# A quarter of the key sums of a decode attention moved from TensorE to ScalarE and VectorE

## The chip, the cores and the metric

The kernel runs on one core of one Trainium2 chip. The metric is device time in microseconds (us) of one execution, so lower is better. Each kernel was run several times, and one execution of each was recorded by the hardware profiler. All profile times below count from the first recorded instruction. The profiled span is some 1.8 to 2.1 us shorter than the device time of the same run.

## The reference

One token (D = 640) passes a pre-norm attention block and then a gated feed-forward block. The attention reads the last 4096 keys and values of 32 heads of 192 numbers, all in bfloat16.

```python
W = min(4096, max(256, Sk // 4))                 # 4096
q = (norm(x) @ wq).reshape(B, Sq, 32, 192).transpose(0, 2, 1, 3)
k = k_cache[:, :, Sk - W:, :]
v = v_cache[:, :, Sk - W:, :]
scores = jnp.einsum('bhqd,bhkd->bhqk', q, k) * Dh ** (-0.5)
o = jnp.einsum('bhqk,bhkd->bhqd', softmax(scores), v)
h = x + merge_heads(o) @ wo
z = gelu(norm(h) @ w_in)                         # 640 -> 1536, halves z1 and z2
out = h + (z1 * (w_sp * norm(z2) + b_sp)) @ w_out    # 768 -> 640
```

The caches that are read are 2 x 32 x 4096 x 192 x 2 bytes = 100.7 MB, and the weights some 18.7 MB more. Each byte is used once.

## The kernel before

A *pair* is two heads. The 16 pairs have one K tile and one V tile each, of 128 partitions x 12288 bfloat16 (3.1 MB). All loads are issued by one engine, SyncE, in one fixed order, and a load is issued when a buffer of its kind is free. There are six buffers for K and V together and two for wo.

```python
plan = [...wq..., K0, K1]
for t_ in range(NP):                                   # NP = 16 pairs
    if t_ + 2 < NP: plan.append(K[t_ + 2])
    if t_ % 2 == 1 and t_ < NP - 1: plan.append(wo[t_ // 2])
    plan.append(V[t_])
plan += [wo[7], w_in in 4 pieces, w_out in 6 pieces]
def free(kind, n=1):
    live[kind] -= n
    issue()                    # issues loads until the next one has no free buffer
```

The scores of a pair are made in two halves of 32 keys per partition. VectorE multiplies the keys by q in place, TensorE adds groups of products by matmuls with an identity matrix (12 for each half, 384 in all), and VectorE adds the last 16 columns of each key out of PSUM.

```python
def multiply(t, ch):           # VectorE, 128 x 6144 products
    nc.vector.tensor_tensor(out=kc, in0=kc, in1=q2[:, t:t + 1, :].to_broadcast([P, JC, Dh]), op=ALU.mult)

def contract(t, ch):           # TensorE; G = 16, NT = 12
    for n in range(NT):
        nc.tensor.matmul(psv, lhsT=ident_bf[:], rhs=k3[:, ch * JC:(ch + 1) * JC, n * G:(n + 1) * G],
                         start=(n == 0), stop=(n == NT - 1))
    if ch == NCH - 1:
        free("kv")             # the K buffer is free when TensorE has read it

def collect(t, ch):            # VectorE, 128 x 512 -> 128 x 32
    nc.vector.tensor_reduce(out=S[:, ch * JC:(ch + 1) * JC], in_=st[t]["ps"][ch], axis=AX.X, op=ALU.add)
```

Then come a maximum over the head (`head_max`), the exponentials on ScalarE (`exps`), the products with V on TensorE (`values`), the softmax sums Z of two pairs (`sums`, `norms`) and the projection with wo (`project`). The first six of the eight groups q of wo give rows of the result and the last two give columns. The stages of neighbouring pairs are interleaved:

```python
for t in range(NP):
    multiply(t, 0); collect(t - 1, 1); norms(...); multiply(t, 1)
    contract(t, 0); head_max(t - 1); scaled(t - 3); columns2(...)
    values(t - 2, vt, 0, J // 2); collect(t, 0); exps(t - 1, ...); project(...)
    contract(t, 1); values(t - 2, vt, J // 2, J); free("kv"); sums(...)
```

The *tail* after the loop handles the last two V tiles, adds the rows and x into columns (`fold`), and does the whole feed-forward block. Its end is this:

```python
    rstd2 = ln_rstd(hv2)       # start value, then two Newton steps, tiny VectorE instructions
    z2_ps = half_in(Fh)        # w_in, gelu, second norm with rstd3 = ln_rstd(hv3), ...
    nc.vector.tensor_tensor(out=gv[:], in0=z1[:], in1=gz[:], op=ALU.mult)
    for c in range(FHC):       # 6 pieces of w_out, 4 matmuls each
        for g in range(NG):
            nc.tensor.matmul(orow[...], lhsT=gv[:, c:c + 1], rhs=w_out_sb[:, c, g * OW:(g + 1) * OW], ...)
    nc.vector.tensor_copy(out=o_sb[:], in_=orow)      # the eviction
    nc.sync.dma_start(out=out[...], in_=o_sb[0::32, :])
```

## Time and profile before

| | before |
|---|---|
| device time | 287.45 us median of 4 runs (287.22 to 288.01) |
| profiled span | 285.7 us |
| packet time of the load queue | 97.4% of 16 engines' span = 278.3 us |
| PE, VectorE, ScalarE busy | 184.7, 193.0, 26.4 us |
| mean granted TensorE clock | 0.865 |

These are lines of the page of the kernel before. The first ones give the busy time of each engine, the granted clock in 40 slices, two DMA queues (packets, MB, share of 16 engines' span) and the chain that ended last, by engine. The L lines are groups of instructions: busy us and mean ns of one, then the idle time of the engine ahead of them and what ended most of it. The last two lines are loads: KB each and median us from issue to landing.

```profile
span 285.7 us, 3043 instructions
...
PE 184.7 (65%) x1245; PEld 77.2 (27%) x1245; DVE 193.0 (68%) x282; ACT 26.4 (9%) x98; POOL 2.3 (1%) x10
...
PEclk9999998889999579968997797978898679979555
...
q1 hardware_dynamic: 5544, 119.35, 97.4%
q8 instruction: 10, 0.16, 0.2%
...
DMA 59%; PE 20%; DVE 19%; issue 1%; SPq 1%; DVEq 0%
...
L299 PE MATMUL sc_ps<-k_t,ident_bf 128*128 128x512 bf16 x384 | 109.0, 445 | 45.6 <-DVE k_t L293 45.6
L293 DVE TENSOR_TENSOR k_t<-k_t,q_203 128x6144 bf16<-128x6144 bf16 x32 | 107.2, 3353 | 35.9 <-DMA k_t<-in_A_k_cache_dram 35.9
...
L332 ACT ACTIVATE E_125<-S,bias 128x64 bf16<-128x64 f32 x12 | 4.2, 360 | 73.8 <-DVE bias L326 73.8
...
k_t<-in_A_k_cache_dram SPq DMA_DIRECT2D x15, 3072.0 KB, 31.4
v_t<-in_A_v_cache_dram SPq DMA_DIRECT2D x15, 3072.0 KB, 31.6
...
```

The load queue q1 is busy 97.4% of the span, and no engine has more than 68%. VectorE waits 35.9 us in all for K tiles (group L293), so in the loop the arithmetic waits for the data. A K load lands 31.4 us after its issue.

The end of the chain of waits before, in order of time (start, us, what):

```profile
...
264.60 11.96 DMA w_in_sb<-in_B_w_in_dram
...
276.57 5.74 DMA w_out_sb<-in_B_w_out_dram
...
282.35 0.33 PE sc_ps L572 x4
...
282.71 0.33 DVE o_sb L575
```

At the end the chain runs along loads: the last landing of w_out at 276.57 + 5.74 = 282.31 us releases the last four matmuls, and the eviction of the result starts at 282.71 us. The rest, eviction and store, takes 2.8 to 3.0 us in every kernel here. So the start of the eviction is a good measure of the end, and I use it below.

### The profile page before, as it was taken

What the parts mean: (1) busy time and instruction counts of PE and PEld (TensorE: products, weight loads), DVE (VectorE), ACT (ScalarE), POOL (GpSimd) and SP (SyncE); (2) the same over time, 40 slices, a digit from 0 to 9 for tenths busy, and PEclk for the clock granted to TensorE, in tenths of its full rate; (3) what the DMA queues carried; (4) which work ended last, traced back from release to release, by engine and by line L of the source; (5) the groups of instructions that cost most, each with busy time, mean ns of one, the idle gap of its engine ahead of it and who ended that gap; (6) DMA issues with size and microseconds to landing.
All of it is one profiled execution on the core that took longest, in us unless ns stands there. A gap on an engine that the chain in (4) does not pass through costs nothing.

```text
span 285.7 us, 3043 instructions
## 1 busy us (share of the span) xinstructions
PE 184.7 (65%) x1245; PEld 77.2 (27%) x1245; DVE 193.0 (68%) x282; ACT 26.4 (9%) x98; POOL 2.3 (1%) x10
## 2 busy tenths in 40 slices
PE   1229948779765766736573866655772776776973
PEld 0003413223222322312231322212221222323562
DVE  7300088989996849587595939595786849986342
ACT  2001200101102010201002010201010010202211
POOL 3000000000000000000000000000000000000000
PEclk9999998889999579968997797978898679979555
DMA  8999999999999999999999999999999999999992
GB/s 330 406 434 434 434 440 416 421 452 440 443 434 406 440 420 434 420 463 440 434 429 414 420 440 428 445 445 440 427 411 417 434 434 418 479 434 390 394 403 95
DMA packets 5564, 119.54 MB, mean 418 GB/s; under 512 B 1005, under 2 KB 2286, under 8 KB 2990
## 3 DMA queue, kind: packets, MB, share of 16 engines
q1 hardware_dynamic: 5544, 119.35, 97.4%
q8 instruction: 10, 0.16, 0.2%
q14 instruction: 4, 0.03, 0.0%
q10 hardware_dynamic: 6, 0.00, 0.0%
HBM read 119.34 MB, written 0.00 MB: 418 GB/s over the span
## 4 chain that ended last, share of the span: by engine, by line
DMA 59%; PE 20%; DVE 19%; issue 1%; SPq 1%; DVEq 0%
DMA k_t<-in_A_k_cache_dram 35%; DVE k_t L293 13%; PE sc_ps L299 12%; DMA v_t<-in_A_v_cache_dram 11%; DMA wq_t<-in_A_wq_dram 7%; PE sc_ps L265 5%; DMA w_in_sb<-in_B_w_in_dram 4%; DVE ob L395 2%; DMA w_out_sb<-in_B_w_out_dram 2%; DVE S L307 2%; PE pv_169 L370 1%; SPq L60 1%; PE sm_ps L317 1%; PE attn_ps L428 1%; DVE gm L319 0%
## 5 line engine op out<-in xcount | busy, mean ns | idle before, releaser
L299 PE MATMUL sc_ps<-k_t,ident_bf 128*128 128x512 bf16 x384 | 109.0, 445 | 45.6 <-DVE k_t L293 45.6
L293 DVE TENSOR_TENSOR k_t<-k_t,q_203 128x6144 bf16<-128x6144 bf16 x32 | 107.2, 3353 | 35.9 <-DMA k_t<-in_A_k_cache_dram 35.9
L299 PEld LDWEIGHTS <-ident_bf 128*128 128x128 bf16 x384 | 41.2, 111 | 104.0 <-issue 63.3
L265 PE MATMUL sc_ps<-wq_t,xn_128 128*128 128x512 bf16 x60 | 18.3, 467 | 10.8 <-DMA wq_t<-in_A_wq_dram 8.4
L307 DVE TENSOR_REDUCE S<-sc_ps 128x32 f32<-128x512 f32 x32 | 21.9, 683 | 1.9 <-PE sc_ps L299 1.9
L273 DVE COPY sp_f<-sm_ps 128x2 f32<-128x2 f32 x1 | 0.2, 159 | 26.6 <-PE sm_ps L271 26.6
L265 PEld LDWEIGHTS <-xn_128 128*128 128x128 bf16 x60 | 6.7, 112 | 22.1 <-issue 15.0
L332 ACT ACTIVATE E_125<-S,bias 128x64 bf16<-128x64 f32 x12 | 4.2, 360 | 73.8 <-DVE bias L326 73.8
L332 ACT ACTIVATE E_127<-S,bias 128x64 bf16<-128x64 f32 x10 | 3.5, 363 | 67.0 <-DVE bias L326 67.0
L332 ACT ACTIVATE E_126<-S,bias 128x64 bf16<-128x64 f32 x10 | 3.5, 362 | 66.7 <-DVE bias L326 66.7
L319 DVE TENSOR_REDUCE gm<-sm_ps 2x1 f32<-2x128 f32 x16 | 4.5, 278 | 7.6 <-PE sm_ps L317 7.6
L370 PE MATMUL pv_169<-v_t,E_127 128*8 128x512 bf16 (+1 forms) x72 | 7.9, 489 | 1.9 <-DMA v_t<-in_A_v_cache_dram 1.9
L370 PE MATMUL pv_171<-v_t,E_126 128*8 128x512 bf16 (+1 forms) x72 | 6.2, 425 | 1.1 <-DMA v_t<-in_A_v_cache_dram 1.1
L267 ACT ACTIVATE q_203<-sc_ps 128x512 bf16<-128x512 f32 x6 | 3.6, 597 | 29.9 <-PE sc_ps L265 29.9
L370 PE MATMUL pv_169<-v_t,E_125 128*8 128x512 bf16 (+1 forms) x72 | 6.2, 425 | 0.0
L370 PEld LDWEIGHTS <-E_127 128*8 128x8 bf16 (+1 forms) x120 | 3.5, 87 | 8.1 <-issue 6.0
L370 PE MATMUL pv_171<-v_t,E_125 128*8 128x512 bf16 (+1 forms) x48 | 4.2, 424 | 1.5 <-DMA v_t<-in_A_v_cache_dram 1.5
L370 PE MATMUL pv_171<-v_t,E_127 128*8 128x512 bf16 (+1 forms) x48 | 4.1, 424 | 1.3 <-DMA v_t<-in_A_v_cache_dram 1.3
L370 PEld LDWEIGHTS <-E_125 128*8 128x8 bf16 (+1 forms) x120 | 3.2, 84 | 6.3 <-issue 3.6
L370 PEld LDWEIGHTS <-E_126 128*8 128x8 bf16 (+1 forms) x120 | 3.2, 84 | 6.0 <-issue 3.3
L370 PE MATMUL pv_169<-v_t,E_126 128*8 128x512 bf16 (+1 forms) x48 | 4.2, 425 | 0.0
L326 DVE TENSOR_TENSOR bias<-off,sm_ps 128x2 f32<-128x2 f32 x16 | 2.4, 148 | 2.5 <-PE sm_ps L324 2.5
(225 smaller groups left out, 141.5 us busy)
## 6 DMA issues: line engine op xcount, KB each, us to landing
k_t<-in_A_k_cache_dram SPq DMA_DIRECT2D x15, 3072.0 KB, 31.4
v_t<-in_A_v_cache_dram SPq DMA_DIRECT2D x15, 3072.0 KB, 31.6
wq_t<-in_A_wq_dram SPq DMA_DIRECT2D x5, 1536.0 KB, 14.2
wo_t<-in_A_wo_dram SPq DMA_DIRECT2D x7, 960.0 KB, 20.3
k_t<-in_A_k_cache_dram SPq DMA_DIRECT2D x1, 1536.0 KB
v_t<-in_A_v_cache_dram SPq DMA_DIRECT2D x1, 1536.0 KB
w_in_sb<-in_B_w_in_dram SPq DMA_DIRECT2D x2, 576.0 KB, 14.4
wo_t<-in_A_wo_dram SPq DMA_DIRECT2D x2, 480.0 KB, 13.4
```

What stands on the lines that cost most here:

```text
L60: eng.add_instruction(mybir.InstDMACopy(name=nc.get_next_instruction_name(), mode="Copy", queue="qSPDynamicHW", ins=eng.lower_ap_dma(in_, ...
L265: nc.tensor.matmul(psv, lhsT=xn2[:, c, a, :], rhs=wc[:, gq:gq + 4, a, w0:w0 + P], start=(c == 0 and a == 0), stop=(c == DC - 1 and a == 1))
L267: nc.scalar.activation(out=q2f[:, gq:gq + 4, w0:w0 + P], in_=psv, func=ACT.Copy, scale=scale)
L293: nc.vector.tensor_tensor(out=kc, in0=kc, in1=q2[:, t:t + 1, :].to_broadcast([P, JC, Dh]), op=ALU.mult)
L299: nc.tensor.matmul(psv, lhsT=ident_bf[:], rhs=k3[:, ch * JC:(ch + 1) * JC, n * G:(n + 1) * G], start=(n == 0), stop=(n == NT - 1))
L307: nc.vector.tensor_reduce(out=S[:, ch * JC:(ch + 1) * JC], in_=st[t]["ps"][ch], axis=AX.X, op=ALU.add)
L317: nc.tensor.transpose(out=mT[0:2, 0:P], in_=m2[:], identity=ident_f[:])
L319: nc.vector.tensor_reduce(out=gm[:], in_=mT[0:2, 0:P], axis=AX.X, op=ALU.max)
L332: nc.scalar.activation(out=E[:, :, a], in_=S[:], func=ACT.Exp, bias=bias[:, a:a + 1], accum_out=zq[q][:, a, b:b + 1])
L370: nc.tensor.matmul(pv[p0:p0 + 2 * n, :].rearrange("p (k r i) -> p k r i", k=n, r=32), lhsT=E[:, j0:j0 + n, :].rearrange("p j a -> p (j a)" ...
L395: nc.vector.tensor_reduce(out=ob[:, i0:i0 + ni], in_=flat.rearrange("p (k r i) -> p i r k", k=n, i=ni), axis=AX.X, op=ALU.add)
L428: nc.tensor.matmul(rows[p0:p0 + 1, :], lhsT=o[:, i:i + 1], rhs=wo_t[:, c0:c0 + DH2], start=(q == 0 and i < 2), stop=(q == NR - 1 and i >= ...
```

## The change

The intent was to take work from TensorE, which was 65% busy, and to give it to engines with room. It has four parts:

1. In 13 of 16 pairs a quarter of the keys, 16 per partition, is no longer added by TensorE: in 7 pairs ScalarE adds them with one Copy with a sum for each key, and in 6 pairs VectorE adds them with one reduction over 16 x 192 products. 78 of 384 identity matmuls go.
2. The softmax sums Z are made for two q at once.
3. The wo group q6 gives rows too, and x joins the rows.
4. The fold of the rows moves from before the last two V tiles to amid the last V tile.

The diff also moves one small matmul of the tail, the one that feeds the last norm, ahead of those that add h to the result.

```diff
+    BY_ACT = (0, 1, 3, 5, 7, 9, 11)
+    BY_DVE = (2, 4, 6, 8, 10, 12)
+    def add_on_act(t, part):
+        ...
+        for j in range(j0, j0 + JS // 2):
+            nc.scalar.activation(out=k3[:, j, :], in_=k3[:, j, :], func=ACT.Copy, accum_out=S[:, j:j + 1])
+    def add_on_dve(t):
+        nc.vector.tensor_reduce(out=st[t]["S"][:, J - JS:J], in_=products(t)[:, J - JS:J, :], axis=AX.X, op=ALU.add)
     def contract(t, ch):
-        for n in range(NT):
+        j0, j1 = pe_keys(t, ch)                # 32 keys, or 16 where another engine adds the rest
+        g = 512 // (j1 - j0)
+        for n in range(Dh // g):               # 12 matmuls, or 6
-        if ch == NCH - 1:
-            free("kv")
...
         if t < NP - 1:
             contract(t, 1)
+            if t in BY_ACT:
+                add_on_act(t, 1)
+            if t in BY_DVE:
+                add_on_dve(t)
+            free("kv")
...
+    def sums2(q): ...      # Z of two q in one matmul of eight columns
-    NR = NQ - 2
+    NR = NQ - 1            # q6 as rows
...
-    fold(rows_sb)          # ahead of the last but one V
...
-    values(NP - 1, vt, 0, LAST[-2])
+    values(NP - 1, vt, 0, LAST[-3])
+    fold(rows_sb)
+    values(NP - 1, vt, LAST[-3], LAST[-2])
```

More of the change, by code (lines that the diff above doesn't have):

```diff
@@ L49 @@
     NCH = J // JC
-    G = 512 // JC
-    NT = Dh // G
     KVE = J * Dh
     NWQ = (DC + 1) // 2
-    assert 2 * HD == KVE and J % JC == 0 and Dh % G == 0 and H % 4 == 0 and Dh % 6 == 0
+    assert 2 * HD == KVE and J % JC == 0 and Dh % (1024 // JC) == 0 and H % 4 == 0 and Dh % 6 == 0
     NE16 = 32
@@ L201 @@
         nc.vector.tensor_scalar(out=sel[h_][:], in0=par[:], scalar1=half[:, h_:h_ + 1], scalar2=None, op0=ALU.mult)
+    quarter = const.tile([P, 2, 2], F32)
+    for h_ in range(4):
+        nc.vector.tensor_reduce(out=quarter[:, h_ // 2, h_ % 2:h_ % 2 + 1], in_=ident_f[:, 32 * h_:32 * h_ + 32], axis=AX.X, op=ALU.add)
     blocks = const.tile([P, 2, 8], F32)
@@ L276 @@
     attn_ps = psum.tile([P, 512], F32, tag="acc", name="attn_ps", bufs=1)
-    DH2 = D // 2
-    rows = attn_ps[:, DC + 3:DC + 3 + DH2]
+    CUT = (0, 3 * P, D)
+    rows = attn_ps[:, DC + 3:DC + 3 + CUT[1]]
     nc.vector.memset(rows, 0.0)
@@ L282 @@
     zq = {}
+    zpair = {}
     o_last = []
@@ L286, with pe_keys, products @@
     st = {}
+    JS = JC // 2
+    BY_ACT = (0, 1, 3, 5, 7, 9, 11)
+    BY_DVE = (2, 4, 6, 8, 10, 12)
+    def pe_keys(t, ch):
+        lo, hi = ch * JC, (ch + 1) * JC
+        if ch == 0 and t in BY_ACT:
+            hi -= JS
+        if ch == 1 and t in BY_DVE:
+            hi -= JS
+        return lo, hi
+    def products(t):
+        return st[t]["k"][:].rearrange("p (j d) -> p j d", d=Dh)
+    def add_on_act(t, part):
+        k3, S = products(t), st[t]["S"]
+        j0 = JC - JS + part * JS // 2
+        for j in range(j0, j0 + JS // 2):
+            nc.scalar.activation(out=k3[:, j, :], in_=k3[:, j, :], func=ACT.Copy, accum_out=S[:, j:j + 1])
+    def add_on_dve(t):
+        nc.vector.tensor_reduce(out=st[t]["S"][:, J - JS:J], in_=products(t)[:, J - JS:J, :], axis=AX.X, op=ALU.add)
     def multiply(t, ch):
@@ L295, in contract @@
     def contract(t, ch):
-        k3 = st[t]["k"][:].rearrange("p (j d) -> p j d", d=Dh)
-        psv = sc_bank()[:, 0:JC * G].rearrange("p (j g) -> p j g", j=JC)
-        for n in range(NT):
-            nc.tensor.matmul(psv, lhsT=ident_bf[:], rhs=k3[:, ch * JC:(ch + 1) * JC, n * G:(n + 1) * G],
-                             start=(n == 0), stop=(n == NT - 1))
+        j0, j1 = pe_keys(t, ch)
+        g = 512 // (j1 - j0)
+        psv = sc_bank()[:].rearrange("p (j g) -> p j g", g=g)
+        for n in range(Dh // g):
+            nc.tensor.matmul(psv, lhsT=ident_bf[:], rhs=products(t)[:, j0:j1, n * g:(n + 1) * g],
+                             start=(n == 0), stop=(n == Dh // g - 1))
         st[t]["ps"][ch] = psv
-        if ch == NCH - 1:
-            free("kv")
     def collect(t, ch):
         S = st[t]["S"]
-        nc.vector.tensor_reduce(out=S[:, ch * JC:(ch + 1) * JC], in_=st[t]["ps"][ch], axis=AX.X, op=ALU.add)
+        j0, j1 = pe_keys(t, ch)
+        nc.vector.tensor_reduce(out=S[:, j0:j1], in_=st[t]["ps"][ch], axis=AX.X, op=ALU.add)
         if ch == NCH - 1:
@@ L327, in exps @@
         q, b = divmod(t, 2)
-        if b == 0:
-            zq[q] = small.tile([P, 2, 2], F32, tag="Z", name="Z")
+        if b == 0 and q % 2 == 0 and q < NQ - 2:
+            z4 = small.tile([P, 2, 2, 2], F32, tag="Z", name="Z")
+            zq[q], zq[q + 1] = z4[:, 0], z4[:, 1]
+            zpair[q] = z4
+        elif b == 0 and q not in zq:
+            zq[q] = small.tile([P, 2, 2], F32, tag="Z1", name="Z1")
         E = E_bufs[t % NE]
@@ L343, in sums, with sums2, norms2 @@
         return Z_ps
+    def sums2(q):
+        Z_ps = bank()
+        nc.tensor.matmul(Z_ps[:, 0:8], lhsT=ones_f[:], rhs=zpair.pop(q)[:].rearrange("p k a b -> p (k a b)"), start=True, stop=True)
+        return Z_ps
+    def norms2(q, Z_ps):
+        r8 = small.tile([P, 2, 2, 2], F32, tag="r8", name="r8")
+        nc.vector.reciprocal(out=r8[:], in_=Z_ps[:, 0:8].rearrange("p (k a b) -> p k a b", k=2, a=2))
+        rm = small.tile([P, 2, 2, 2], F32, tag="rm", name="rm")
+        nc.vector.tensor_tensor(out=rm[:], in0=r8[:], in1=quarter[:, None, :, :].to_broadcast([P, 2, 2, 2]), op=ALU.mult)
+        rh = small.tile([P, 2, 2], F32, tag="rh2", name="rh2")
+        nc.vector.tensor_reduce(out=rh[:], in_=rm[:], axis=AX.X, op=ALU.add)
+        for k_ in range(2):
+            rzq[q + k_] = rh[:, k_]
     def norms(q, Z_ps):
@@ L422, in project @@
             nc.vector.tensor_scalar(out=o[:], in0=oT[:, 0:RQ], scalar1=rz[:, 0:1], scalar2=None, op0=ALU.mult)
+        if q == 0:
+            for h_ in range(2):
+                nc.tensor.matmul(rows[64 * h_:64 * h_ + 1, 0:CUT[h_ + 1] - CUT[h_]], lhsT=ones_bf[0:1, 0:1],
+                                 rhs=x_row[0:1, CUT[h_]:CUT[h_ + 1]], start=True, stop=False)
         for i in range(RQ):
@@ L426, in project @@
                     p0 = 32 * (i % 2) + 64 * h_
-                    c0 = i * D + h_ * DH2
-                    nc.tensor.matmul(rows[p0:p0 + 1, :], lhsT=o[:, i:i + 1], rhs=wo_t[:, c0:c0 + DH2],
-                                     start=(q == 0 and i < 2), stop=(q == NR - 1 and i >= RQ - 2))
+                    nc.tensor.matmul(rows[p0:p0 + 1, 0:CUT[h_ + 1] - CUT[h_]], lhsT=o[:, i:i + 1],
+                                     rhs=wo_t[:, i * D + CUT[h_]:i * D + CUT[h_ + 1]],
+                                     start=(q == 0 and i == 1), stop=(q == NR - 1 and i >= RQ - 2))
             else:
@@ L437, in fold @@
     def fold(rows_sb):
-        for c in range(DC):
-            nc.tensor.matmul(attn_ps[:, c:c + 1], lhsT=x_row[0:1, c * P:(c + 1) * P], rhs=ones_bf[0:1, 0:1],
+        n = CUT[1] // P
+        for c in range(n):
+            w = 2 if c + n < DC else 1
+            nc.tensor.matmul(attn_ps[:, c:c + n * (w - 1) + 1:n], lhsT=rows_sb[:, c * P:(c + 1) * P], rhs=halfsel[:, 0:w],
                              start=(c == 0), stop=False)
-        for c in range(DC):
-            for h_ in range(2):
-                lo, hi = max(c * P, h_ * DH2), min((c + 1) * P, (h_ + 1) * DH2)
-                if lo < hi:
-                    nc.tensor.matmul(attn_ps[lo - c * P:hi - c * P, c:c + 1],
-                                     lhsT=rows_sb[:, lo - h_ * DH2:hi - h_ * DH2], rhs=halfsel[:, h_:h_ + 1],
-                                     start=False, stop=False)
-    NR = NQ - 2
+    NR = NQ - 1
     assert NCH == 2
@@ L453 @@
         multiply(t, 0)
+        if t in BY_ACT:
+            add_on_act(t, 0)
         if s_on:
@@ L456 @@
         if v_on and t % 2 == 1:
-            norms((t - 2) // 2, Z_ps)
+            q = (t - 2) // 2
+            if q >= NQ - 2:
+                norms(q, Z_ps)
+            elif q % 2 == 1:
+                norms2(q - 1, Z_ps)
         multiply(t, 1)
@@ L479 @@
             contract(t, 1)
+            if t in BY_ACT:
+                add_on_act(t, 1)
+            if t in BY_DVE:
+                add_on_dve(t)
+            free("kv")
         if v_on:
@@ L483 @@
         if s_on and t % 2 == 0:
-            Z_ps = sums((t - 1) // 2)
-    rows_sb = const.tile([P, DH2], F32)
-    nc.scalar.copy(out=rows_sb[:], in_=rows)
+            q = (t - 1) // 2
+            if q >= NQ - 2:
+                Z_ps = sums(q)
+            elif q % 2 == 1:
+                Z_ps = sums2(q - 1)
     collect(NP - 1, 1)
@@ L498 @@
     project(NQ - 2, oT)
+    rows_sb = const.tile([P, CUT[1]], F32)
+    nc.scalar.copy(out=rows_sb[:], in_=rows)
     scaled(NP - 2)
@@ L544 @@
                                    accum_out=sums3[:, 1:2])
+    lin_ps = bank()[:, 0:2]
+    nc.tensor.matmul(lin_ps, lhsT=rootF_f[:], rhs=sums3[:], start=True, stop=True)
     for g in range(NG):
@@ L550 @@
                                  rhs=ident_f[:, lo - c * P:hi - c * P], start=(lo == g * OW), stop=False)
-    lin_ps = bank()[:, 0:2]
-    nc.tensor.matmul(lin_ps, lhsT=rootF_f[:], rhs=sums3[:], start=True, stop=True)
     m3 = small.tile([P, 2], F32, tag="lnm", name="lnm")
```

## The prediction

> **What bounds the kernel now.** The load queue. The page's DMA part: 119.35 MB, packet time worth 97.4% of 16 engines' span, 278.3 us of 285.7. The chain of waits has its first data at 3.3 us and the last landing (w_out) at 282.3 us, a window of 279.0 us. So the queue stands still for about 0.7 us in all. The large packets in the trace (49152 bytes, median 1815 ns, 16 engines) move at 433 GB/s[...]. After the last landing come 4 matmuls, an eviction and the store: 3.4 us.
>
> Nothing else is near its limit: PE 65%, VectorE 68%, ScalarE 9%. VectorE waits 35.9 us for K tiles (table of groups).
>
> **What the change does.** Every load stays: same bytes, descriptors, order.
> - Removed: 6 of 24 identity matmuls in 13 K pairs, 78 of 384. At 230 to 430 ns each (timeline, full clock and throttled): 18 to 33 us of PE.
> - VectorE, 6 pairs: a reduction of 16 x 192 products. The PSUM reduction of 512 takes 683 ns; an estimate from that is 3.3 to 4 us each, 20 to 24 us in all. A pair now takes VectorE about 12 us of the 15.7 us that its loads take: 15 to 16 us in these pairs, 12 in the others; the average fits.
> - ScalarE, 7 pairs: 16 Copy activations with sums. Exp of 64 with its accumulator read repeats each 0.34 us (timeline); for 192 elements I estimate 0.45 us: 7 us a pair, 50 us in all, on an engine that waits over 200 us for VectorE.
> - Z of two q at once, x as a row: a microsecond or two, in slack.
>
> K buffers come free 2 to 5 us later. A K or V load lands 31 us after issue (DMA issues), its own transfer 7.3 us: about 24 us of queued work stand ahead of it. A late free eats reserve, not time.
>
> **The tail** is the closest race. The last wo load is issued at 259.7 us, when project(5) frees its buffer; the queue then holds about 5 us of V. Project(5) is fixed by the last K's landing. After the last V piece, compute (gv at 281.1 us, then matmuls) ends within 0.4 us of where w_out's landing ends it. The fold moves into the last V, where PE waits for pieces anyway; q6 as rows costs what its columns cost (about 1 us). A better clock there only exposes w_out's landing.
>
> **Critical path:** of the PE work removed, practically nothing. Predicted 287.2 us, 8 in 10 between 286.6 and 287.9. Faster by over 2%: 0.01; within: 0.97; slower: 0.02.
>
> **What would show it.** Queue at 97 to 98% and about 418 GB/s; last w_out landing at 282 +- 0.6 us; PE busy 155 to 168 us; VectorE 210 to 217 us, its waits for K shorter; ScalarE 70 to 85 us; issue to landing 26 us or more.
>
> **What would make it wrong.** VectorE's reduction at twice my estimate, so that the queue runs dry (issue to landing falling toward 7 us); ScalarE holding K buffers beyond 24 us; the last wo issued after 264 us; the fold pushing gv beyond w_out's landing; or a queue whose rate depends on what engines do in SBUF, which one trace can't show.

## More of the kernel before

The queue q8 carries ten packets of 16384 bytes that are no data at all (the page lists its kind as `instruction`).

## The result

| | before | after |
|---|---|---|
| device time, median | 287.45 us (287.22 to 288.01, 4 runs) | 286.86 us (286.71 to 287.31, 4 runs) |
| ratio, 95% interval | | 0.9979 (0.996 to 0.9998) |
| profiled span | 285.7 us | 285.0 us |
| mean granted clock | 0.865 | 0.818 |

A ratio in this document is the mean time of one kernel's fast runs over the mean of the other's fast runs of the same rounds, so it isn't quite the ratio of the medians. The change is the same within 2%, and a tight look at this pair says 0.6 us faster. The repeat on another chip (`after_same` below, 0.9981 with an interval of 0.9958 to 1.0003) agrees in size but doesn't exclude that nothing was gained.

The page after, the lines that answer to those shown of before:

```profile
span 285.0 us, 3082 instructions
...
PE 170.7 (60%) x1134; PEld 67.3 (24%) x1134; DVE 212.3 (74%) x289; ACT 64.1 (22%) x316; POOL 2.3 (1%) x10
...
PEclk9999996889599755985698759956896679999595
...
q1 hardware_dynamic: 5544, 119.35, 97.7%
q8 instruction: 9, 0.15, 0.2%
...
DMA 40%; DVE 38%; PE 18%; issue 2%; SPq 1%; ACT 0%; DVEq 0%; ACTq 0%
...
L325 PE MATMUL sc_ps<-k_t,ident_bf 128*128 128x512 bf16 x306 | 91.7, 459 | 45.6 <-DVE k_t L318 45.6
L318 DVE TENSOR_TENSOR k_t<-k_t,q_208 128x6144 bf16<-128x6144 bf16 x32 | 107.1, 3350 | 15.0 <-DMA k_t<-in_A_k_cache_dram 14.6
...
L308 ACT ACTIVATE k_t<-k_t 128x192 bf16<-128x192 bf16 x112 | 38.8, 347 | 34.1 <-DVE k_t L318 34.1
...
L311 DVE TENSOR_REDUCE S<-k_t 128x16 f32<-128x3072 bf16 x6 | 20.1, 3345 | 0.0
...
k_t<-in_A_k_cache_dram SPq DMA_DIRECT2D x15, 3072.0 KB, 27.8
v_t<-in_A_v_cache_dram SPq DMA_DIRECT2D x15, 3072.0 KB, 30.6
...
```

The work moved as planned. The loads are the same 5544 packets. TensorE lost 78 identity matmuls (group L325) and 14.0 us, VectorE gained 19.3 us and ScalarE 37.7 us. VectorE's reduction takes 3.35 us (L311) and one key on ScalarE 0.347 us (L308). VectorE's wait for K fell from 35.9 to 14.6 us (L318), and in the chain VectorE went from 19% to 38%. The granted clock fell with the work: a mean of 0.818 after 0.865, and 0.639 in the experiment that takes away most of the identity matmuls (`few_sums`). Why it falls, the traces don't show. An identity matmul takes 459 ns after 445 in these two profiles, but 444 in `after_same` (clock 0.834) and 467 in `null_before` (0.844), so this difference is no larger than that between two profiles of one kernel; in `few_sums` it is 593.

The end of the chain of waits after, in order of time:

```profile
...
280.36 0.30 DVE gz L624
...
280.75 0.17 DVE gv L629
...
280.97 1.01 PE sc_ps L632 x18
282.01 0.33 DVE o_sb L635
```

Before, a landing released the last matmuls. Now the chain runs through arithmetic: gv at 280.75 us, 18 matmuls, the eviction at 282.01 us. The eviction comes 0.70 us earlier, which is the whole gain of the span. So the question is small but sharp. The same bytes went through a queue that was busy all the time in both kernels. Why does the data end 0.64 us earlier (last w_out packet at 281.26 us after 281.90)?

### The profile page after: what moved, and what is told of

Same layout as the page of the kernel before. It is cut to its first block, busy times and chain, and to the rows that moved or that the text cites. A ratio compares the mean times of both kernels' runs of the same rounds, so it can differ in the third digit from the quotient of the medians.

```text
span 285.0 us, 3082 instructions
## 1 busy us (share of the span) xinstructions
PE 170.7 (60%) x1134; PEld 67.3 (24%) x1134; DVE 212.3 (74%) x289; ACT 64.1 (22%) x316; POOL 2.3 (1%) x10
## 3 DMA queue, kind: packets, MB, share of 16 engines
q1 hardware_dynamic: 5544, 119.35, 97.7%
## 4 chain that ended last, share of the span: by engine, by line
DMA 40%; DVE 38%; PE 18%; issue 2%; SPq 1%; ACT 0%; DVEq 0%; ACTq 0%
DVE k_t L318 20%; DMA k_t<-in_A_k_cache_dram 20%; DMA v_t<-in_A_v_cache_dram 9%; PE sc_ps L325 8%; DMA wq_t<-in_A_wq_dram 6%; PE sc_ps L266 5%; DMA wo_t<-in_A_wo_dram 5%; DVE S L311 5%; DVE ob L439 4%; DVE S L332 3%; PE attn_ps L475 1%; SPq L58 1%; PE sm_ps L342 1%; DVE gm L344 1%; DVE m L335 1%
## 5 line engine op out<-in xcount | busy, mean ns | idle before, releaser
L325 PE MATMUL sc_ps<-k_t,ident_bf 128*128 128x512 bf16 x306 | 91.7, 459 | 45.6 <-DVE k_t L318 45.6
L318 DVE TENSOR_TENSOR k_t<-k_t,q_208 128x6144 bf16<-128x6144 bf16 x32 | 107.1, 3350 | 15.0 <-DMA k_t<-in_A_k_cache_dram 14.6
L325 PEld LDWEIGHTS <-ident_bf 128*128 128x128 bf16 x306 | 32.8, 112 | 96.0 <-issue 62.3
L308 ACT ACTIVATE k_t<-k_t 128x192 bf16<-128x192 bf16 x112 | 38.8, 347 | 34.1 <-DVE k_t L318 34.1
L332 DVE TENSOR_REDUCE S<-sc_ps 128x32 f32<-128x512 f32 (+1 forms) x32 | 21.8, 682 | 4.4 <-PE sc_ps L325 4.4
L308 ACT ACTIVATION_READ_ACCUMULATOR k_t<-k_t 128x1 f32 x112 | 20.9, 186 | 0.0
L311 DVE TENSOR_REDUCE S<-k_t 128x16 f32<-128x3072 bf16 x6 | 20.1, 3345 | 0.0
L266 PEld LDWEIGHTS <-xn_128 128*128 128x128 bf16 x60 | 6.7, 112 | 21.6 <-issue 14.6
L414 PE MATMUL pv_174<-v_t,E_127 128*8 128x512 bf16 (+1 forms) x72 | 7.9, 489 | 3.1 <-DMA v_t<-in_A_v_cache_dram 3.1
L414 PE MATMUL pv_176<-v_t,E_126 128*8 128x512 bf16 (+1 forms) x72 | 7.3, 459 | 2.3 <-DMA v_t<-in_A_v_cache_dram 2.3
L414 PE MATMUL pv_176<-v_t,E_125 128*8 128x512 bf16 (+1 forms) x48 | 5.6, 509 | 1.1 <-DMA v_t<-in_A_v_cache_dram 1.1
L414 PE MATMUL pv_174<-v_t,E_125 128*8 128x512 bf16 (+1 forms) x72 | 6.2, 425 | 0.0
L414 PEld LDWEIGHTS <-E_127 128*8 128x8 bf16 (+1 forms) x120 | 3.4, 89 | 8.3 <-issue 6.4
L414 PEld LDWEIGHTS <-E_126 128*8 128x8 bf16 (+1 forms) x120 | 3.4, 86 | 7.6 <-issue 5.2
L414 PE MATMUL pv_176<-v_t,E_127 128*8 128x512 bf16 (+1 forms) x48 | 5.0, 472 | 0.2 <-DMA v_t<-in_A_v_cache_dram 0.2
## 6 DMA issues: line engine op xcount, KB each, us to landing
k_t<-in_A_k_cache_dram SPq DMA_DIRECT2D x15, 3072.0 KB, 27.8
w_in_sb<-in_B_w_in_dram SPq DMA_DIRECT2D x2, 576.0 KB, 14.6
```

Of the source, the lines that this page charges most:

```text
L266: nc.tensor.matmul(psv, lhsT=xn2[:, c, a, :], rhs=wc[:, gq:gq + 4, a, w0:w0 + P], start=(c == 0 and a == 0), stop=(c == DC - 1 and a == 1))
L308: nc.scalar.activation(out=k3[:, j, :], in_=k3[:, j, :], func=ACT.Copy, accum_out=S[:, j:j + 1])
L311: nc.vector.tensor_reduce(out=st[t]["S"][:, J - JS:J], in_=products(t)[:, J - JS:J, :], axis=AX.X, op=ALU.add)
L325: nc.tensor.matmul(psv, lhsT=ident_bf[:], rhs=products(t)[:, j0:j1, n * g:(n + 1) * g], start=(n == 0), stop=(n == Dh // g - 1))
L332: nc.vector.tensor_reduce(out=S[:, j0:j1], in_=st[t]["ps"][ch], axis=AX.X, op=ALU.add)
L414: nc.tensor.matmul(pv[p0:p0 + 2 * n, :].rearrange("p (k r i) -> p k r i", k=n, r=32), lhsT=E[:, j0:j0 + n, :].rearrange("p j a -> p (j a)" ...
```

## The experiments

Each experiment ran beside the kernel before on one chip; the chip of the first pair isn't on record. The first and third groups shared chip 1, the second was on chip 11. In the three groups the kernel before has medians of 288.15, 288.21 and 288.28 us, so times of different groups are best compared by ratios.

### Group 1: which half of the change is it?

My first theory was that the new tail (parts 2 to 4) makes the gain and that the moved key sums are neutral. The rival was that less TensorE work makes it.

**The kernel before, unchanged** (`null_before`), to see what nothing at all looks like. No edit.

> The kernel before, unchanged, timed against itself: it measures what a ratio of 1 looks like. Queue theory (the load queue decides everything up to its last landing, and the 0.6 us of the change come from the last few microseconds): ratio 0.9990 to 1.0010, queue share 97 to 98%, last w_out landing at 281.6 to 282.4 us; how far the last load engine trails the others will differ from the run before, where it was 0.8 us. If the landing here is at 281.7 or earlier and the kernel is as fast as the changed one, the gain was chance.

Measured: 288.25 us, ratio 1.0004 (0.999 to 1.0017). Its profiled span is 286.4 us where the first profile of the same kernel had 285.7, so single spans scatter by 0.7 us, as much as the effect. A span alone settles nothing here. Its last w_out load landed at 283.02 us, later than the 281.6 to 282.4 that I had expected.

**Only the key sums moved** (`keys_only`), on the kernel before:

```diff
+    BY_ACT = (0, 1, 3, 5, 7, 9, 11)
+    BY_DVE = (2, 4, 6, 8, 10, 12)
+    ... pe_keys, add_on_act, add_on_dve, contract and collect as in the change; sums, project, fold as before
```

> Only the key sums moved to ScalarE and VectorE; Z, wo rows, fold and tail as before. Queue theory: nothing, ratio 0.999 to 1.001 (287.2 to 287.7 us), though PE busy falls by 10 to 20 us and VectorE rises by 20. Rival, the freed PE (less throttled in the tail, or less contention in SBUF, so a faster queue): ratio 0.9985 or lower, and the whole gain of the change is here.

Measured: 288.08 us, ratio 0.9993 (0.9976 to 1.0011).

**All but the key sums** (`no_keys`), on the kernel after:

```diff
-    BY_ACT = (0, 1, 3, 5, 7, 9, 11)
-    BY_DVE = (2, 4, 6, 8, 10, 12)
+    BY_ACT = ()
+    BY_DVE = ()
```

> The whole change but the key sums: all keys on PE. Queue theory with the gain in the tail: this alone gives the gain, ratio 0.997 to 0.999, gv not later than 281.0 us. Rival of the freed PE: ratio 0.9995 to 1.0005.

Measured: 288.20 us, ratio 0.9992 (0.9976 to 1.0008). I had expected the gain here, and it isn't here: the theory of the tail falls, at least as the whole reason. Neither half alone differs from the kernel before, though either interval would also allow most of the gain.

**Two of twelve identity matmuls only** (`few_sums`), on the kernel before. Its sums are wrong; the comparison with the reference passed all the same, which says how little its tolerance sees of the scores.

```diff
-        for n in range(NT):
+        for n in range(0, NT, NT - 1):
```

> Wrong result on purpose: the kernel before with 2 of 12 identity matmuls in each key sum, 320 of 384 fewer, four times what the change removes. Queue theory: PE busy falls by 70 to 95 us and the clock is granted more, yet the time falls by at most 0.8 us (ratio 0.997 to 1.000), all of it in the last 5 us; queue share 97 to 98%. Rival of the freed PE: over 1.5 us faster, the load rate up.

Measured: 287.46 us, ratio 0.9979 (0.9965 to 0.9993), and TensorE busy 132.1 us. I had expected TensorE's busy time to fall by 70 to 95 us and its clock to rise; it fell by 53 us, and the mean granted clock fell to 0.639. The ratio is the one of the whole change, with none of its other parts. Four times as many matmuls were taken away (320 of 384 instead of 78), and the gain isn't four times as large. These are lines of its page and of the end of its chain of waits:

```profile
...
PE 132.1 (46%) x925; PEld 44.9 (16%) x925; DVE 193.0 (68%) x282; ACT 26.3 (9%) x98; POOL 2.3 (1%) x10
...
q8 instruction: 7, 0.11, 0.2%
...
```

```profile
...
281.41 0.18 DVE gv L569
...
281.63 1.00 PE sc_ps L572 x24
282.65 0.33 DVE o_sb L575
```

It has 7 packets on q8 in place of 10, and its end, too, is arithmetic (gv at 281.41 us) and no longer a landing. The eviction at 282.65 us is 0.76 us earlier than in `null_before` (283.41), which ran on the same chip, but only 0.06 us earlier than in the first profile of the kernel before (282.71), since gv came 0.55 us later than there.

### What the packet records show

The trace records each packet of each DMA queue: start, duration, size. Three readings of all profiles together gave the theory that the second group tests.

*The queue was neither faster nor slower.* A data packet of 49152 bytes has the same median, 1815 ns, before and after, and packet time summed over the queue is 278.3 and 278.4 us of 16 engines. Between 5 and 278 us, a stretch of 273 us, the packet times add up to 273.5 us for each engine in both (neighbouring small packets overlap a little in the records), so hardly any time is left in which an engine stands idle. With one such packet on each of the 16 engines, 16 x 49152 bytes in 1815 ns are 433 GB/s.

*The 16 engines end apart.* The last packets of w_out (5120 bytes, 0.196 us each) end at these times, in us, from the packet records:

```
before       ... 281.01 281.04 281.08 281.09 281.30 281.49 281.70 281.90
null_before  ... 281.07 281.20 281.27 281.47 281.67 281.86 282.07 282.27 282.47 282.67
after_pad    ... 281.10 281.10 281.19 281.38 281.58 281.78 281.98 282.18 282.39 282.59
after        ... 281.06 281.07 281.09 281.11 281.19 281.26
```

In the unchanged kernel's second profile eight packets come one after the other, 0.2 us apart: one engine works off its share alone, while 15 are done. The view by stretches of time shows the same. Its columns are the stretch, its length, busy us and instructions of five engines, the granted clock, the DMA share and GB/s. First the kernel before unchanged (`null_before`), then the kernel after:

```profile
...
core 0: us, PE busy (x) PEld busy (x) DVE busy (x) ACT busy (x) POOL busy (x), PEclk, DMA share, GB/s
...
281.20:281.60 0.40, 0.00 (x0) 0.00 (x0) 0.10 (x1) 0.27 (x1) 0.00 (x0) 0.50 0.06 26
281.60:282.00 0.40, 0.28 (x12) 0.28 (x13) 0.06 (x1) 0.00 (x0) 0.00 (x0) 0.50 0.06 26
282.00:282.40 0.40, 0.40 (x16) 0.16 (x5) 0.00 (x0) 0.00 (x0) 0.00 (x0) 0.50 0.06 26
...
```

```profile
...
core 0: us, PE busy (x) PEld busy (x) DVE busy (x) ACT busy (x) POOL busy (x), PEclk, DMA share, GB/s
...
280.80:281.20 0.40, 0.23 (x11) 0.23 (x13) 0.12 (x1) 0.00 (x0) 0.00 (x0) 0.50 0.39 143
281.20:281.60 0.40, 0.40 (x20) 0.39 (x9) 0.00 (x0) 0.00 (x0) 0.00 (x0) 0.50 0.00 0
281.60:282.00 0.40, 0.36 (x12) 0.09 (x3) 0.00 (x0) 0.00 (x0) 0.00 (x0) 0.50 0.00 0
...
```

A share of 0.06 is one engine of 16. In the kernel before it lasts to 282.67 us; in the kernel after there is nothing on the DMA engines from 281.26 us. The matmuls wait for the last engine. The trace records 16 landings for each load, and in `null_before` those of one load lie up to 3.8 us apart near the end. In the first profile of the kernel before the last packet ends at 281.90 us, the last landing comes at 282.31, and the last four matmuls start at 282.35.

*An engine becomes late at an instruction fetch.* The 16 landings of a load keep their distances from the median for tens of us, from load to load. They change at the packets of q8. These carry 16384 bytes each, start on average once in 249 to 275 recorded TensorE instructions (matmuls and weight loads), depending on the kernel, and take 0.88 to 1.10 us in the profiles of the table below. That they fetch TensorE's instructions is a reading: the page lists q8 as `instruction`, and their number follows that of the matmuls, 7 packets with 925 of them (`few_sums`), 8 with 1098 (`more_act`), 9 with 1134 to 1212 and 10 with 1245 or 1246. In `null_before` a fetch starts at 276.80 us. The three latest of the 16 landings of a load, in us from the median of the 16, just before and after it:

```
load with median 275.02 us:  +0.57 +0.72 +0.73
load with median 277.46 us:  +0.59 +0.74 +2.25
load with median 279.24 us:  +0.58 +0.75 +2.18
load with median 280.46 us:  +0.54 +0.71 +2.16
```

One engine gets 1.5 us later than the latest before, and stays so to the end (+2.25, +2.18, +2.16 us over three us of loads). That a queue with 97% packet time left it no gap to catch up in is a reading and was not tested. In the kernel before the fetch at 277.18 us takes the latest landing from +0.67 (load at 277.42) to +1.46 us (279.26). In the kernel after two fetches differ. One starts at 275.68 us and falls on an early engine: the latest landing is +0.80 us before and +0.68 after it. The next starts at 280.96 us, when nearly all data is in.

This can be checked on every fetch that has loads landing before and after it. Of 88 such fetches in the eleven profiles of the table below, 81 set exactly one of the 16 landings back, by 1.35 to 1.65 us, while the other 15 keep their distances. That is more than the 0.9 to 1.1 us that the fetch itself takes; why, the records don't say.

Theory: the change took 111 matmuls with their weight loads from TensorE's instruction stream, so one fetch less falls into the loaded time, and the last one comes too late to hurt. The gain is the lone engine. Rival: less TensorE work, at a lower clock, somehow frees the data path.

### Group 2: the number of instructions

**The kernel after again** (`after_same`), on another chip. No edit.

> The changed kernel, unchanged, beside the others of this call. Ratio to before 0.997 to 0.999. Fetch theory (each 16 KB block of PE's instructions[...] is fetched by one load engine, which runs about 1 us late from then on; the ninth block falls on an engine that is already late, and that engine ends the queue last): the ninth fetch starts after 280.5 us, when the queue is nearly empty, and no load engine trails the others by more than 0.5 us at the end. Rival, the PE work itself: nothing said about fetches.

Beside the sizes in this theory stand those measured above: packets of 16384 bytes that take 0.88 to 1.10 us and set a landing back by 1.35 to 1.65 us.

Measured: 287.71 us, ratio 0.9981 (0.9958 to 1.0003), on the first value. But six runs go from 287.0 to 288.72, so the gain isn't there in every execution. Only one of the six was profiled (span 285.2 us, the second fastest), but the record has the granted clock of each: 0.828 and 0.834 in the two fastest, 0.809 in the next two, then 0.798 and 0.792. That would fit an end set by arithmetic that a lower clock delays. The four runs of the first pair don't show it (the fastest had the lowest clock, 0.800), so it is a lead and not shown.

**The kernel after with 112 one-element matmuls** (`after_pad`). They give TensorE back its number of matmuls (1246) with next to no work:

```diff
         mT = bank()
+        for _ in range(7):
+            nc.tensor.matmul(mT[0:1, 256:257], lhsT=ones_bf[0:1, 0:1], rhs=ones_bf[0:1, 0:1], start=True, stop=True)
```

> The changed kernel with 7 matmuls of one element in each of 16 pairs, 112 in all, so that PE has as many instructions as before (1246 matmuls) and about 10 us more busy time, in idle time. Fetch theory: the ninth fetch comes back to about 277 us, one engine ends its w_out packets 0.7 to 1.6 us behind the rest, the gain is gone: ratio to before 0.9995 to 1.001. Rival (less PE work on the real chain, better clock in the tail, shorter tail): the gain stays, ratio 0.997 to 0.999.

Measured: 288.06 us, ratio 0.9988 (0.9969 to 1.0007), below the 0.9995 to 1.001 that I had expected. The times of this kernel and of `after_same` overlap, and time alone doesn't decide. The trace tells more: ten fetches on q8 as before, one of them at 276.72 us, a lone engine to 282.59 us, and an end that is a landing again. Its stretches and the end of its chain of waits:

```profile
...
core 0: us, PE busy (x) PEld busy (x) DVE busy (x) ACT busy (x) POOL busy (x), PEclk, DMA share, GB/s
...
281.20:281.60 0.40, 0.00 (x0) 0.00 (x0) 0.17 (x1) 0.18 (x1) 0.00 (x0) 0.50 0.06 26
281.60:282.00 0.40, 0.37 (x12) 0.35 (x13) 0.00 (x0) 0.00 (x0) 0.00 (x0) 0.50 0.06 26
282.00:282.40 0.40, 0.40 (x12) 0.09 (x4) 0.00 (x0) 0.00 (x0) 0.00 (x0) 0.50 0.06 26
...
```

```profile
...
276.65 6.29 DMA w_out_sb<-in_B_w_out_dram
...
282.98 0.33 PE sc_ps L634 x4
...
283.33 0.32 DVE o_sb L637
```

All the key sums are where the change put them, and the span is that of the kernel before (286.3 against 285.7 and 286.4 us). The one-element matmuls were enough to bring the lone engine back. Two cautions: the profile is that of the slowest of the six runs, where the one of `after_same` is of the second fastest; and the arithmetic came later too (gv at 281.41 us after 280.75 and 280.98). By the rule below it alone would have put the eviction at 282.66 us, so of the 1.3 us between this eviction and that of `after` the lone engine accounts for the last 0.67.

**Few sums with 320 one-element matmuls** (`few_sums_pad`):

```diff
+        for _ in range(20):
+            nc.tensor.matmul(mT[0:1, 256:257], lhsT=ones_bf[0:1, 0:1], rhs=ones_bf[0:1, 0:1], start=True, stop=True)
```

> Wrong result on purpose: the kernel before with 2 of 12 identity matmuls in each key sum, which gave 0.9979, plus 20 matmuls of one element in each of 16 pairs, so that the number of PE instructions is that of before and the work far less. Fetch theory: ten fetches again, the ninth near 277 us, a late engine at the end, ratio 0.9995 to 1.001. Rival (freed PE): ratio stays at 0.997 to 0.9985.

Measured: 288.91 us, ratio 1.002 (1.0002 to 1.0038), above the range that I had expected, so slower than the kernel before while TensorE has 44 us less work. The lone engine is back (fetch at 278.92 us, last packet 282.74 us after 281.34). But this run isn't a clean one: gv came at 282.89 us, with TensorE at half clock from 249 us to the end, and its arithmetic ended last. By the rule below the queue alone would have given an eviction at 283.5 us instead of 284.1.

**All 13 pairs on ScalarE** (`more_act`), which takes away 36 more matmuls; 6 pairs use both engines:

```diff
-    BY_ACT = (0, 1, 3, 5, 7, 9, 11)
+    BY_ACT = tuple(range(13))
```

> A version that might beat both: the changed kernel with ScalarE taking its quarter in all 13 pairs, so 36 fewer matmuls and about 192 more ScalarE instructions. Fetch theory: the ninth PE fetch falls after the last load or away, so it is at least as fast as the changed kernel, ratio to before 0.996 to 0.998; ScalarE's own fetches (8 KB, some 0.3 to 0.4 us each on one engine) may take part of it back. ScalarE rises to about 115 us busy and must not hold K buffers: issue to landing stays above 25 us.

Measured: 288.02 us, ratio 0.9999 (0.9974 to 1.0024). The queue did what the theory asks (8 fetches, last packet 281.55 us, no lone engine), but gv came 1.6 us later than in the kernel after (282.38 against 280.75 us). It doesn't beat the change, and the expected 0.996 to 0.998 was missed. The packets that I took for ScalarE's fetches are those of q14, also listed as `instruction`: 4 in the kernel before with 98 ScalarE instructions, 6 in the kernel after with 316, 8 here with 508. In the spans of the kernels before and after they carry 8192 bytes and take 0.309 us each. What they cost here was not separated. TensorE had half clock from 266 to 273 us, but half clock alone doesn't explain the delay: the kernel before had it from 263.4 us to its end, and there gv came at 280.86. What made gv late here is open.

### The profiles with equal loads in one table

Times in us; the last row is a kernel of group 3. "Fetch" is the start of the ninth fetch on q8, or of the last one before the data ended where there was no ninth by then (few_sums seventh, more_act eighth); the rule in the last column is the later of (last packet + 0.75) and (gv + 1.25), two constants that I read from these traces: the first is landing and four matmuls, the second 24 matmuls.

| kernel | matmuls | fetch | last packet | gv starts | eviction starts | rule |
|---|---|---|---|---|---|---|
| before | 1245 | 277.18 | 281.90 | 280.86 | 282.71 | 282.65 |
| null_before | 1245 | 276.80 | 282.67 | 281.50 | 283.41 | 283.42 |
| keys_only | 1167 | 280.55 | 282.40 | 281.14 | 283.22 | 283.15 |
| no_keys | 1212 | 279.11 | 282.73 | 280.86 | 283.47 | 283.48 |
| after_pad | 1246 | 276.72 | 282.59 | 281.41 | 283.33 | 283.34 |
| few_sums_pad | 1245 | 278.92 | 282.74 | 282.89 | 284.13 | 284.14 |
| few_sums | 925 | 279.27 | 281.34 | 281.41 | 282.65 | 282.66 |
| after | 1134 | 280.96 | 281.26 | 280.75 | 282.01 | 282.01 |
| after_same | 1134 | 281.38 | 281.45 | 280.98 | 282.22 | 282.23 |
| more_act | 1098 | 278.80 | 281.55 | 282.38 | 283.62 | 283.63 |
| newton1 | 1134 | 280.98 | 280.99 | 280.39 | 281.86 | 281.74 |

The upper six have had nine fetches well before their data ends, and a trailing engine: last packet 281.90 to 282.74 us. In the lower five the ninth fetch starts after 280.9 us or there is none before the data ends: 280.99 to 281.55. In the upper group the ninth fetch starts before 280.6 us. Fetches seven and eight can come just as late (few_sums, more_act) without harm. The landings also tell the place among the 16 of the engine that the ninth fetch set back. In `null_before`, `no_keys`, `after_pad` and `few_sums_pad` it was among the three latest, and the data ends at 282.59 to 282.74 us. In `before` and `keys_only` it stood in the middle (ninth to twelfth), and the data ends at 281.90 and 282.40. So the two profiles of the same kernel differ by where the fetch fell. The reading that fits is that the first eight fall on different engines and the ninth on one that was hit before; the records don't say which engine carried a packet, so this reading is inferred from the landings.

The table also suggests why the halves gave nothing, with one profile for each. `no_keys` has its ninth fetch at 279.11 us and `keys_only` at 280.55, both still in time to hit a loaded engine. It takes both halves to push it past 280.9 us.

### Group 3: reserve and queue

**w_out loaded once more, amid the V loads** (`extra_load`), 0.98 MB more than the kernel after. This is the positive control for "the queue bounds":

```diff
+        if t_ == 8:
+            for c in range(FHC):
+                plan.append(("w", lambda c=c: load(w_out_sb[:, c, :], wout_v[c])))
```

> The changed kernel, with the six w_out loads issued once more in the middle of the V loads: 0.98 MB more, 192 packets of 5120 bytes at 196 ns, so 2.35 us of each load engine. No arithmetic is added. Queue theory: the whole 2.35 us show, span 287.3 to 287.9 us, ratio to before 1.005 to 1.008. Rival (engines or the chain of K and V arithmetic bound the kernel, the queue has room): under 0.5 us.

Measured: 290.06 us, ratio 1.0065 (1.0043 to 1.0088), about 1.9 us over the kernel before. Its packets are 192 x 0.196 us over 16 engines = 2.35 us of queue, and the last data packet comes at 283.59 us, 2.1 to 2.3 us later than in the two profiles of the kernel after. Loaded bytes show in full at the queue's end. The ratio is as expected; the profiled span, 288.8 us, is above the expected 287.3 to 287.9. In the time a bit is added by arithmetic, which ended this run (gv at 284.71 us), and a bit is taken off by what the kernel after gains over before.

**The VectorE reduction of keys done twice, and three times** (`dve_x2`, `dve_x3`), which the prediction's reserve of "about 24 us of queued work" should swallow in large part:

```diff
-        nc.vector.tensor_reduce(out=st[t]["S"][:, J - JS:J], in_=products(t)[:, J - JS:J, :], axis=AX.X, op=ALU.add)
+        for _ in range(2):          # 3 in the other
+            nc.vector.tensor_reduce(out=st[t]["S"][:, J - JS:J], in_=products(t)[:, J - JS:J, :], axis=AX.X, op=ALU.add)
```

> The changed kernel with each of VectorE's 6 key reductions done twice, 20 us more VectorE work on 212. It is the case that the prediction named as its danger. Queue theory with about 20 us of reserve: at most 1 us slower (ratio to before 0.997 to 1.002), issue to landing of K and V falls by some us but stays over 15 us. Rival (VectorE is already the bound of the loop): about 10 to 20 us slower.

> Each of the 6 reductions three times, 40 us more. VectorE has about 28 us of idle time in the loop, so it ends the loop 10 to 20 us late; the last pairs win back some. Reserve theory: 5 to 15 us slower than before, with the loads running out of free buffers or the tail starting late. If there is still no loss, VectorE has far more room than its idle time says.

Measured: 297.49 us, ratio 1.031 (1.0273 to 1.0346), and 314.92 us, ratio 1.0938 (1.091 to 1.0965). Both expectations missed by far: I had 1 us at most for the first and 5 to 15 us for the second, and they cost some 9 and 27 us over the kernel before. Lines of the page of `dve_x2`:

```profile
...
q1 hardware_dynamic: 5544, 119.35, 94.7%
...
L319 DVE TENSOR_TENSOR k_t<-k_t,q 128x6144 bf16<-128x6144 bf16 x32 | 107.1, 3349 | 0.4 <-issue 0.4
...
L312 DVE TENSOR_REDUCE S<-k_t 128x16 f32<-128x3072 bf16 x12 | 40.2, 3351 | 0.2
...
```

VectorE waits for K no more: the idle time ahead of the multiply is 0.4 us after 14.6, and before the change 35.9. VectorE now sets the pace of the loop. The last wo load is issued at 273.98 us instead of 260.00, the queue stands empty for 2.0 us from 273.3, and its share is 94.7%. In `dve_x3`, the third repeat adds another 20.1 us of VectorE and costs 17.4 us, nearly one for one; the queue's share is 90.1%, with gaps of 1.1 to 4.2 us at 155, 189, 226 and 263 us. Yet the median from issue to landing is still 25.0 us for K in `dve_x2` and 22.8 in `dve_x3`, after 27.8. The depth of the queue in the middle hardly tells of the trouble.

**One Newton step less in the two last norms** (`newton1`), on the kernel after, to shorten the arithmetic that ends it:

```diff
-    def ln_rstd(hv):
+    def ln_rstd(hv, steps=2):
...
-        for _ in range(2):
+        for _ in range(steps):
...
-    rstd2 = ln_rstd(hv2)
+    rstd2 = ln_rstd(hv2, 1)
...
-    rstd3 = ln_rstd(hv3)
+    rstd3 = ln_rstd(hv3, 1)
```

> A version that might beat both: the changed kernel with one instead of two Newton steps in the two last norms (relative error of 0.2%, still correct), which takes about 0.8 us out of the tail's arithmetic. The end is the later of queue (last w_out packet + about 0.75 us to the eviction) and arithmetic (gv + 1.25 us). In the changed kernel's two profiles both are within 0.05 us, so profiles like those gain nothing: eviction at 282.0 to 282.3 us, ratio to before 0.997 to 0.9985. Runs in which a low clock makes the arithmetic late gain up to 0.8 us, so the median may fall by 0.2 to 0.4 us.

Measured: 287.01 us (286.90 to 287.05, six runs), ratio 0.9958 (0.9942 to 0.9973), the lowest ratio (its interval overlaps that of `after_same`) and 1.2 us faster than before. Its result passes the comparison with the reference, but `few_sums` showed how tolerant that is, so whoever takes it should look at the precision itself. The end of its chain of waits:

```profile
...
276.50 4.96 DMA w_out_sb<-in_B_w_out_dram
...
281.51 0.33 PE sc_ps L632 x4
...
281.86 0.32 DVE o_sb L635
```

gv now starts at 280.39 us, and a landing ends it again. Its span is 284.9 us, only 0.1 to 0.3 us below that of the kernel after. The two were not timed side by side, so the difference between 0.9958 and 0.998 isn't explained by a test. But the record has the span of every run: 284.8 to 285.3 us for `newton1`, 284.7 to 285.3 in the first four runs of the kernel after, and 285.1 to 286.7 in `after_same`. What `newton1` lacks are the slow runs, at clocks of 0.806 to 0.822. With less arithmetic at the end a low clock may no longer show; that reading is not tested.

## Why the prediction was right or wrong

**"The load queue" bounds the kernel: right.** Same packets, same 278.3 us of packet time, same rate, and 2.35 us of added packets move the queue's end by 2.1 to 2.3 us. Taking 53 us of TensorE's busy time away (`few_sums`) gains no more than taking 14.

**"Of the PE work removed, practically nothing" lies on the critical path: right as to work, and the time of 287.2 us with its range holds.** The work isn't what paid. But the 0.6 us that did come are, by the traces, a term which the sum left out: the *number* of TensorE instructions. A packet of q8 takes 0.88 to 1.10 us, after 81 of 88 of them one of the 16 landings comes 1.35 to 1.65 us later, and the last matmuls start only after the last landing (282.35 us after 282.31 in the kernel before). What shows it: the lone engine in the packet records, in six of the eleven profiles of the table, its appearance at a fetch, and its return with 112 matmuls of one element. What is only inferred: that the packets of q8 are TensorE's instructions and go through the engines of the loads, which engine a fetch uses, and so that the ninth comes back to one that was hit before. In times, the return of the lone engine isn't resolved (0.9988 against 0.9981, intervals overlapping). That 286.86 us lay inside the predicted range is no credit to this term, which the prediction didn't have: the range of 1.3 us is twice the effect.

**"About 24 us of queued work stand ahead of it. A late free eats reserve, not time": the size failed.** The change spent nearly 60% of the real reserve. The reserve that counts is VectorE's waiting for K, 35.9 us before and 14.6 us after; another 20.1 us of VectorE cost 9 us, and the next 20.1 cost 17.4. The sum is a rough measure and not exact: with 14.6 us left, the first 20.1 us should have cost 5.5 us by it, and both together 25.6 where they cost 27. Time from issue to landing counts the queued work at one moment, but an engine that is slower in every pair falls behind pair by pair, and the sum of its waits is about what it has. The change itself stayed inside this reserve, so the predicted time didn't suffer.

**"The tail is the closest race ... w_out's landing ends it": right in kind.** Before, arithmetic would have allowed an eviction at 282.11 us and the queue 282.65 (rule above; gv starts at 280.86 us, and the 281.1 of the prediction is the first matmul that reads it). After, both say 282.01. My sentence that a better tail "only exposes w_out's landing" describes what `newton1` then did.

**The sizes.** VectorE's reduction, estimated at 3.3 to 4 us, takes 3.35. ScalarE's keys, estimated at 0.45 us each, repeat every 0.345 us; so ScalarE has 64.1 us and not 70 to 85. This one was avoidable: in the kernel before, ScalarE's copies of 128 and of 384 elements took 297 ns (L337) and 508 ns (L407), and a line through the two gives an estimate of 350 ns for 192 elements, where the trace has 347. I had scaled up from the Exp of 64 elements instead, which takes 360 ns (L332). The read of the accumulator has a record of its own of 186 ns, which begins some 94 ns before the activation ends, and activation and read together repeat every 0.345 us. What the row would take without the reads was not measured. TensorE has 170.7 us and not 155 to 168 (the repeat has 166.6): 78 fewer identity matmuls, at 459 ns each and a mean granted clock of 0.818 (444 ns and 0.834 in the repeat), after 445 ns and 0.865, or 467 ns and 0.844 in `null_before`. VectorE (212.3), the queue's share and rate (97.7%, 419 GB/s), w_out's landing (281.6 us), the last wo issue (260.0 us) and issue to landing (27.8 us) came as written.

**The risk of "a queue whose rate depends on what engines do in SBUF"** didn't come true: 1815 ns for a packet in both.

Open stays which engine a fetch uses, why some runs of the kernel after lose the gain, and why gv comes late in `more_act` and `few_sums_pad`. The mechanism rests on one profile for each kernel, though on twelve that agree. A kernel with the same number of instructions whose ninth fetch comes at another time was not run.

## What to carry to other kernels

Where a saturated load queue bounded the kernel, as here, work taken off another engine was worth nothing in itself (53 us of TensorE's busy time in `few_sums` gained no more than 14 us in the change). In such a case look at which of the 16 load engines ends last and why: the last packets one by one tell it. Count the instructions of the longest stream as well as their time, since here 81 of 88 fetches set one of the 16 landings back, by 1.35 to 1.65 us. The reserve of an engine beside the queue was here about the sum of its waits for data over the loop, not the depth of the queue; compare added work with that sum before adding it, and leave a margin, since here the cost of too much work was up to 4 us more than the sum says.
